# Reordering group 0's second product, one multiply, and the loads of q and v in a fused pooled-attention and GELU kernel

## Chip, cores, metric

One core of one Trainium2 chip. The metric is device time in microseconds (us) of one execution.

## What is computed

Attention whose keys and values are averaged over groups of 8 positions, then two matrix products with a GELU between them. Cut to what matters:

```python
# q, k, v: (8, 8, 576, 64); w_in: (512, 2048); w_out: (2048, 512), all float32
k_p = k.reshape(B, H, S // 8, 8, D).mean(axis=3)
v_p = v.reshape(B, H, S // 8, 8, D).mean(axis=3)
attn = softmax(q @ k_p^T / sqrt(D))           # 576 x 72 for each batch and head
x = (attn @ v_p) as (4608, 512)               # one row per token
out = gelu_tanh(x @ w_in) @ w_out             # (4608, 512)
```

## The kernel before

The tokens are worked through in nine groups of 512. Each group has a **first product** (64 big matmuls, line L411, and 16 GELUs on ScalarE) and a **second product** (64 big matmuls, L420: four row tiles of 128 tokens by 16 pieces of the sum). Beside the second product of group g runs the attention of batch g + 1, its matmuls put between the big ones at fixed places. Names in the profile: L281, L325 and L310 are scores (L310 those of the last 8 pooled positions, "remainder"), L301 and L336 attention times values, L354 the multiply by the softmax reciprocal, L426 the copy of a finished row tile out of PSUM. The "v sums" add v up over the 8 positions of a pooling group, on VectorE. PE is TensorE, DVE VectorE, ACT ScalarE, SP SyncE, POOL GpSimd.

```python
def load_next():                         # loads of batch g + 2, on GpSimd's queue
    if nb >= KX:                         # KX = 2, nb = g + 1
        nc.gpsimd.tensor_copy(out=gate, in_=eT[64:65, H - 1, 1, 0:2])   # holds the loads back
    ...
    load_k_dma(g + 2)
    ...
    load_v(g + 2, [nc.gpsimd])
    if nb >= KX:
        load_q(g + 2)
```

In groups 2 to 6, SyncE turns the loaded k and q by DMA transposes, k first (L190), then q (L269), each when its data are there. The second product of a group whose next batch is below 2, which is group 0 alone:

```python
at(4, v_half, 1, 0)                      # "at(m, ...)": put ahead of big matmul m
at(18, v_half, 1, 1)                     # second half of the v sums, on VectorE
pos = (6, 14, 21, 27, 34, 41, 48, 55, 61)
for i in range(len(ORDER) + 1):
    ...                                  # cut: at pos[i], scores i into banks 2, 3; values i - 1
                                         # into banks 4, 5 or 6, 7, in turn; exp and reciprocal
    if i:
        at(min(pos[i] + 9, ...), mult, *a)   # frees the two banks of "values i - 1"

seq = [(r, f) for r in range(4) for f in range(4)]      # first quarter of w_out, all row tiles
seq += [(r, 4 * f4 + f) for f4 in range(1, 4) for r in range(2) for f in range(4)]
seq += [(r, f) for r in (2, 3) for f in range(4, FO)]
```

Row tiles 2 and 3 keep the first quarter in banks 6 and 7, which are copied out (L653) so that the attention can have them; the rest of row tile 2 goes into row tile 0's bank, when that has been copied out (L426).

The softmax here doesn't subtract the row's maximum and nothing guards it: scores larger than these inputs give would overflow.

## Time and profile before

| | before |
|---|---|
| median of the first three runs | 301.47 us (301.32 to 301.6) |
| span of the profiled execution | 299.7 us, clock 1.0 |
| group 0's second product, first L420 to first L411 of group 1 | 34.92 to 53.87: 18.95 us |
| L310 of group 2 to L310 of group 3 | 99.29 to 130.63: 31.34 us |
| the same for the groups after | 31.08, 31.07, 31.08 us |

The last two rows are the easiest way to see a hole on an engine that is busy for 98% of the span, as TensorE is: groups 2 to 6 do the same work, so the distance between one instruction and its like in the next group is constant, and what is over 31.08 is a wait.

### The profile page before, as it was taken

Reading aid. Unit: us, or ns where it says so; the run is one execution under the profiler, and the core shown is the slowest. Engines: PE = TensorE matmul, PEld = TensorE weight load, DVE = VectorE, ACT = ScalarE, POOL = GpSimd, SP = SyncE. Lnnn points to the kernel's source line nnn. Section 1 sums busy time; section 2 is a strip of 40 time slices with the busy share of each in tenths; the row PEclk is TensorE's granted clock in tenths of the full one; section 3 lists DMA queues with packets and bytes.
Section 4 is the critical chain, followed back from the end, with each engine's and each line's share of the span. In section 5 each row is a group of like instructions: output and inputs, shape, how many; then the busy total and the mean of one; then the engine's idle time right before and its main releaser. Section 6 shows DMA issues by size and latency. Waiting matters only on the chain.

```text
span 299.7 us, 4384 instructions
## 1 busy us (share of the span) xinstructions
PE 293.4 (98%) x1525; PEld 151.4 (51%) x1525; DVE 153.1 (51%) x311; ACT 216.8 (72%) x408; POOL 38.0 (13%) x69
## 2 busy tenths in 40 slices
PE   8999999999999999999999999999999999999995
PEld 3565555554555455545554555455545555445443
DVE  4787577833675357716691669065924630111112
ACT  1697678879887997889878987798879887206500
POOL 2615100100500060006000410032000000000000
PEclk9999999999999999999999999999999999999999
DMA  7999999870899079846984499629961210121023
GB/s 225 259 225 297 248 216 182 213 146 15 188 264 180 16 171 255 160 77 147 250 180 83 101 258 200 103 50 254 236 120 40 71 37 0 37 70 36 0 54 89
DMA packets 38806, 43.11 MB, mean 144 GB/s; under 512 B 25536, under 2 KB 26176, under 8 KB 38656
## 3 DMA queue, kind: packets, MB, share of 16 engines
q0 software_dynamic: 8016, 24.39, 36.8%
q1 hardware_dynamic: 30064, 17.06, 25.6%
q10 hardware_dynamic: 704, 1.38, 1.4%
q8 instruction: 12, 0.20, 0.3%
q14 instruction: 10, 0.08, 0.1%
HBM read 36.70 MB, written 9.44 MB: 154 GB/s over the span
## 4 chain that ended last, share of the span: by engine, by line
PE 86%; DMA 7%; DVE 2%; issue 1%; POOL 1%; ACT 1%; POOLq 0%; SPq 0%; DVEq 0%
PE PS L411 37%; PE PS L420 36%; DMA qb<-in_q_dram 5%; PE PS L336 3%; PE PS L440 3%; PE PS L325 2%; DMA qT<-qb 2%; PE PS L661 1%; PE PS L281 1%; PE PS L310 1%; PE PS L377 1%; DMA eT<-er 1%; ACT e L288 1%; DVE xT L354 1%; PE PS L301 1%
## 5 line engine op out<-in xcount | busy, mean ns | idle before, releaser
L420 PE MATMUL PS<-w_out_b,gT 128*128 128x512 bf16 x560 | 136.9, 379 | 0.0
L411 PE MATMUL PS<-xT,w_in_b 128*128 128x512 bf16 x576 | 126.2, 379 | 0.0
L417 ACT ACTIVATE gT<-PS 128x512 bf16<-128x512 f32 x144 | 79.3, 609 | 44.3 <-PE PS L411 44.2
L411 PEld LDWEIGHTS <-w_in_b 128*128 128x128 bf16 x576 | 65.1, 113 | 58.8
L420 PEld LDWEIGHTS <-gT 128*128 128x128 bf16 x560 | 53.9, 97 | 51.4 <-issue 2.1
L354 DVE TENSOR_TENSOR xT<-PS,rc 64x288 bf16<-64x288 f32 x112 | 51.0, 455 | 19.7 <-ACT rc L346 17.1
L426 DVE COPY osb<-PS 128x512 f32<-128x512 f32 x33 | 22.8, 692 | 50.2 <-PE PS L420 41.9
L331 ACT ACTIVATE eT<-PS 64x576 bf16<-64x576 f32 x48 | 30.7, 640 | 0.6
L318 DVE COPY eT<-er 8x576 bf16<-8x576 bf16 x24 | 7.3, 303 | 41.4 <-ACT er L316 40.9
L343 ACT ACTIVATE ld<-PS 64x288 f32<-64x288 f32 x56 | 22.6, 403 | 5.8 <-PE PS L336 5.3
L346 ACT ACTIVATE rc<-ld 128x288 f32<-128x288 f32 x56 | 24.8, 443 | 1.8
L388 ACT ACT_TABLE_LOAD x17 | 21.8, 1283 | 3.6 <-issue 3.3
L344 ACT ACTIVATE ld<-PS 64x288 f32<-64x288 f32 x56 | 22.5, 402 | 1.4
L162 DVE TENSOR_TENSOR kt<-kt 128x1280 f32<-128x1280 f32 (+5 forms) x20 | 19.2, 959 | 5.6 <-DMA kt<-in_k_dram 4.9
L336 PE MATMUL PS<-eT,vp 72*128 72x288 bf16 x96 | 19.7, 285 | 0.0
L162 DVE TENSOR_TENSOR vt<-vt 128x512 f32<-128x512 f32 (+2 forms) x18 | 15.6, 865 | 2.7 <-DMA vt<-in_v_dram 2.3
L524 POOL COPY gate<-eT 1x2 bf16<-1x2 bf16 x5 | 0.9, 174 | 123.7 <-DMA eT<-er 123.7
L336 PEld LDWEIGHTS <-vp 72*128 72x128 bf16 x96 | 9.5, 98 | 11.3
L288 ACT ACTIVATE e<-PS 72x576 bf16<-72x576 f32 x16 | 9.9, 643 | 3.8 <-PE PS L281 3.6
L440 PE MATMUL PS<-idle 128*128 128x512 bf16 x31 | 10.0, 474 | 1.2 <-DVE idle L151 1.2
L325 PE MATMUL PS<-qT,kx 128*128 128x288 bf16 x48 | 9.8, 286 | 0.0
L562 DVE COPY kt<-gT 128x512 bf16<-128x512 bf16 x4 | 3.0, 744 | 11.6 <-ACT gT L417 11.6
(67 smaller groups left out, 132.3 us busy)
## 6 DMA issues: line engine op xcount, KB each, us to landing
out_dram<-osb SPq DMA_DIRECT2D x141, 64.0 KB
kt<-in_k_dram POOLq DMA_DIRECT2D x12, 512.0 KB, 7.0
vt<-in_v_dram POOLq DMA_DIRECT2D x12, 512.0 KB, 10.5
qb<-in_q_dram POOLq DMA_DIRECT2D x7, 576.0 KB, 14.8
w_out_b<-in_moe_w_out_dram POOLq DMA_DIRECT2D x4, 512.0 KB, 19.6
w_in_b<-in_moe_w_in_dram POOLq DMA_DIRECT2D x1, 1024.0 KB, 9.3
w_in_b<-in_moe_w_in_dram POOLq DMA_DIRECT2D x2, 512.0 KB, 12.3
kt<-in_k_dram POOLq DMA_DIRECT2D x1, 1024.0 KB, 15.9
```

The source lines that it names most:

```text
L162: nc.vector.tensor_tensor(out=o, in0=a, in1=b, op=ALU.add)
L331: nc.scalar.activation(out=eT[0:64, 2 * pr:2 * pr + 2, c, :], in_=PS[64 * c:64 * c + 64, 2:4, :CH], func=ACT.Exp, scale=1.0 / 64.0)
L336: nc.tensor.matmul(out=PS[:, bank + x, :CH], lhsT=window(vps[b % 2], 2 * pr + x), rhs=eT[:, 2 * pr + x, c, :], start=True, stop=True)
L343: nc.scalar.activation(out=ld[0:64], in_=PS[64:128, bank, :CH], func=ACT.Ln)
L344: nc.scalar.activation(out=ld[64:128], in_=PS[0:64, bank + 1, :CH], func=ACT.Ln)
L346: nc.scalar.activation(out=rc, in_=ld, func=ACT.Exp, scale=-1.0)
L354: nc.vector.tensor_tensor(out=xT[rows, pr, col:col + CH], in0=PS[rows, bank + x, :CH], in1=rc[rows], op=ALU.mult)
L388: nc.scalar.preload_act_table_set(name)
L411: nc.tensor.matmul(out=PS[:, h_bank(g, fo), :], lhsT=w, rhs=xT[:, ko, r0:r0 + GROUP], start=(ko == 0), stop=(ko == KO - 1))
L417: nc.scalar.activation(out=gTs[g][:, fo, :], in_=PS[:, h_bank(g, fo), :], func=ACT.Gelu_apprx_tanh)
L420: nc.tensor.matmul(out=PS[:, bank], lhsT=gTs[g][:, fo, r * 128:(r + 1) * 128], rhs=w_out_b[:, fo], start=(fo == first), stop=(fo == last))
L426: nc.vector.tensor_copy(out=osb, in_=PS[:, bank])
```

## The change

The intent: VectorE should free attention's banks sooner in group 0, and q, which must pass through a transpose, should be on the chip sooner in later groups. `plan` says behind which of the 16 GELUs VectorE gets the next batch's k sums (`kk`) and v sums (`vv`). The multiply with `i == 3` moves from matmul 36 to matmul 34; row tile 0's output copy is queued behind matmul 35, so the multiply passes in front of it.

```diff
-            load_v(g + 2, [nc.gpsimd])
             if nb >= KX:
                 load_q(g + 2)
+            load_v(g + 2, [nc.gpsimd])
...
-                plan = {0: kk, 7: vv[:1], 8: vv[1:]}
+                plan = {0: kk, 11: vv[:1], 12: vv[1:]}
...
-                at(18, v_half, 1, 1)
+                at(12, v_half, 1, 1)
...
-                    at(min(pos[i] + 9, 62 if i < len(ORDER) else 65), mult, *a)
+                    at(min(pos[i] + (7 if i == 3 else 9), 62 if i < len(ORDER) else 65), mult, *a)
...
-            seq = [(r, f) for r in range(4) for f in range(4)]
+            seq = [(r, f) for r in (0, 2, 3, 1) for f in range(4)]
```

## The prediction

> **What bounds the kernel now.** I read the page first, then TensorE's waits, then the timelines around each wait.
>
> ```profile
> span 299.7 us, 4384 instructions
> PE 293.4 (98%) x1525; PEld 151.4 (51%) x1525; DVE 153.1 (51%) x311; ACT 216.8 (72%) x408; POOL 38.0 (13%) x69
> ```
>
> TensorE is occupied for 98% of the span at a granted clock of 1.0, so the change can only give back holes in TensorE's stream. The view of waits, for TensorE alone, has these:
>
> ```profile
> PE PS L440 <- DVE idle L151: 1.2, 1, 1.2
> PE PS L281 <- ACT qT L259: 0.6, 1, 0.6
> PE PS L301 <- DVE xT L354: 0.4, 2, 0.2
> PE PS L310 <- DMA qT<-qb: 0.2, 1, 0.2
> ```
>
> The first two lie in the first 11 us, which the change doesn't touch. The other two (0.6 us together) are what it aims at. The listed waits are a little too small, because a matmul's drawn length overlaps the next one's. Starts are better: a run of 64 big matmuls takes 13.81 us in the chain, 0.216 us each, and an undisturbed pair of L301 (attention times values) delays the next matmul by 0.245 us. TensorE's timeline in group 0's second product:
>
> ```profile
> 42.20 0.41 PE L281 MATMUL PS<-qT,kT 128*72 128x288 bf16 x2
> 42.58 0.28 PE L301 MATMUL PS<-e,vp 72*128 72x288 bf16 x1
> 43.07 0.28 PE L301 MATMUL PS<-e,vp 72*128 72x288 bf16 x1 [0.21 <-DVE xT L354]
> 45.20 1.75 PE L420 MATMUL PS<-w_out_b,gT 128*128 128x512 bf16 x7
> 46.79 0.41 PE L281 MATMUL PS<-qT,kT 128*72 128x288 bf16 x2
> 47.06 0.28 PE L301 MATMUL PS<-e,vp 72*128 72x288 bf16 x1
> 47.55 0.28 PE L301 MATMUL PS<-e,vp 72*128 72x288 bf16 x1 [0.21 <-DVE xT L354]
> ```
>
> First hole: the first L301 starts 0.38 us after the L281 pair instead of 0.25 (0.13 lost), and the second 0.49 us after the first instead of 0.12 (0.37 lost): **0.50 us**. Second hole: again 0.37, plus 0.02, plus 0.08 in the run at 45.20, which took 1.75 us where other runs of seven take 1.67: **0.47 us**. Why is in VectorE's timeline:
>
> ```profile
> 38.18 0.69 DVE L653 COPY osb<-PS 128x512 f32<-128x512 f32 x1
> 39.53 0.69 DVE L653 COPY osb<-PS 128x512 f32<-128x512 f32 x1 [0.67 <-PE PS L420]
> 40.26 1.15 DVE L162 TENSOR_TENSOR vt<-vt 128x512 f32<-128x512 f32 x2
> 41.44 0.60 DVE L162 TENSOR_TENSOR vp<-vt 64x128 bf16<-64x128 f32 x2
> 42.08 1.92 DVE L354 TENSOR_TENSOR xT<-PS,rc 64x288 bf16<-64x288 f32 x4
> 45.83 0.69 DVE L426 COPY osb<-PS 128x512 f32<-128x512 f32 x1 [1.84 <-PE PS L420]
> 46.55 0.94 DVE L354 TENSOR_TENSOR xT<-PS,rc 64x288 bf16<-64x288 f32 x2
> ```
>
> VectorE works in program order: partial copy of row tile 2, partial copy of tile 3 (it waits 0.67 us for TensorE), second half of the v sums, and only then, at 42.08, the multiplies that free the banks of the next L301 pair. At 46.55 the multiply stands behind an output copy.
>
> The third hole is in group 3. A row-tile run of two ends and L310 (remainder scores) waits for the transposed q; the SyncE timeline gives the cause, beside group 5 as one that doesn't wait:
>
> ```profile
> 122.67 1.32 SPq L190 DMA_TRANSPOSE kx<-kz  x1
> 125.97 2.67 SPq L269 DMA_TRANSPOSE qT<-qb  x1
> ...
> 185.09 1.31 SPq L190 DMA_TRANSPOSE kx<-kz  x1
> 186.50 4.36 SPq L269 DMA_TRANSPOSE qT<-qb  x1
> ```
>
> L310 starts 0.79 us after the L420 pair before it (129.84 to 130.63), against 0.53 in group 2 (98.76 to 99.29): **0.26 us**. In group 3 the transpose of q can't be issued at 124.0, when that of k is done, but at 125.97, when q lands (the chain of waits has q's load there, 15.80 us, then 4.61 us of transpose).
>
> [...]the bar at 125.97 is 2.67 us, the landing comes after 4.61.[...] the trace has 692 for the output's add and a mean of 455 for L354.[...]
>
> **The change part by part.** It adds and removes no instruction. The order of instructions, old against new, differs on GpSimd (q before v, five groups), on VectorE in one place (in group 0 two multiplies move in front of an output copy), and on TensorE in the row tile that a matmul takes. The new places of the v sums (11 and 12 for 7 and 8, 12 for 18) change no engine's order, so I count zero for them.
>
> 1. Row tiles 0, 2, 3, 1. Tiles 2 and 3 finish their quarter after matmuls 7 and 11 instead of 11 and 15. Matmul 11 ended at about 38.14 (the copy began at 38.18). VectorE finishes the first half of the v sums at 38.11, copies tile 2 to 38.87 and tile 3 to 39.59 without a wait, does the second half of the v sums (1.79 us) to 41.40, and two multiplies to 42.35 (their reciprocal was there at 40.83). L301 needs them at 42.45 and 42.57. The first hole closes: **-0.50 us**, with a thin margin of 0.2 us.
>
> 2. The multiply in front of the copy. ScalarE is occupied without a break from 38.85 to 44.70 and isn't sped up, so the reciprocal for this multiply still comes at 44.70. Multiplies 44.74 to 45.68. The copy of row tile 0, ready at 45.32 now, runs behind them, 45.72 to 46.41. Row tile 2's next matmul uses that bank. It would start at 46.00 (0.50 sooner than an undisturbed 46.50) but must wait for about 46.46. So at this point 0.45 of part 1 is lost again, TensorE being 0.11 ahead of the old 46.57. Then L301 finds its banks free: 0.37 and some hundredths saved. Part 1 and 2 together: 0.11 + 0.37 = **-0.48 us**, not 0.97. From there ScalarE's and VectorE's chains move along by the same amount; I find no later wait (the next multiply is done at 48.1, needed at 48.9).
>
> 3. q before v. Its issue moves up by the 1.28 us of the two v issues, and its data no longer queue behind 1 MB of v. q should land before k's transpose is issued, so q's goes out right behind, as in group 5: 6.35 us before L310 there, against 4.66 in group 3, 5.66, 5.80 and 6.02 in groups 2, 4 and 6. The transpose took 4.61, so none waits: **-0.26 us**. v lands last, when q did: 125.97 in group 3 instead of before 122.66. Its sums take 2.8 us on VectorE, to 128.8; they are first needed by L336 at 133.6, and VectorE's next other work is at 132.63. No cost.
>
> Sum: -0.48 - 0.26 = -0.74 us. 301.47 - 0.74 = **300.7 us**.
>
> **The rivals.**
> - *Both holes of group 0 close and no copy waits* (the reciprocal comes sooner than I think, or the bank is free earlier): -0.97 - 0.26, 300.2 us. Against it: ScalarE's unbroken row up to 44.70.
> - *The reordering only moves the wait*: the copy behind the multiply holds the bank for as long as the multiply did, and part 1's margin of 0.2 us proves too thin. Group 0 gains 0 to 0.2, in all 301.1 to 301.4 us. For it: VectorE's work between 38 and 46.5 is the same, in another order.
> - *The transposes collide with v.* The first transpose of q, issued at 46.42 among other loads, landed at 54.16, after 7.7 us. With 7.7 us and issue 6.35 us ahead, L310 would wait 1.4 us in each of five groups: plus 7 us, 308 us. Against it: v ends at about the time at which q ended before, so at most 2 us of the transpose overlaps, and the margin is 6.35 - 4.61 = 1.7 us.
> - *q was hidden anyway.* Four of five groups show no wait, so part 3 may be worth 0.0 in the timed runs: 301.0 us.
>
> **Range and chances.** 300.7 is the sum; the low end of 300.1 is the first rival with a little of the runs' spread (301.32 to 301.6), the high end of 301.5 is the second and the fourth together. 2% is 6 us, five times all the holes that can be closed, so faster by that is next to impossible; slower needs the collision in every group.
>
> **What would show it.** In the new profile: the copies of tiles 2 and 3 back to back from 38.2, the first multiply at about 41.4, no wait at the L301 pair near 42.5; the output copy at about 45.7 and a hole of 0.4 us ahead of the matmul that follows (row tile 2, near 46.4), put down to that copy; no hole at the L301 near 46.9; group 1 starting near 53.5 instead of 54.03. In groups 2 to 6 q's transpose starts within 0.2 us of the end of k's issue and L310 has no wait for it; VectorE waits about 3 us for v without TensorE noticing. The prediction is wrong if TensorE waits for v's sums at L336, if L310 waits in several groups, or if group 0 gains under 0.2 or over 0.9 us.

## The result

300.82 us (median of 6, 300.5 to 301.21) against 301.39 (median of 6, 301.09 to 301.65). Ratio 0.9982, 95% interval 0.9969 to 0.9994: 0.18%, or 0.54 us. Ratios here are of means, so they are not quite the ratio of the medians quoted beside them.

The page of the kernel after, its first lines, and TensorE's waits after:

```profile
span 299.1 us, 4388 instructions
PE 293.1 (98%) x1525; PEld 151.3 (51%) x1525; DVE 153.3 (51%) x311; ACT 216.7 (72%) x408; POOL 38.1 (13%) x69
```

```profile
PE PS L440 <- DVE idle L151: 1.2, 1, 1.2
PE PS L281 <- ACT qT L259: 0.6, 1, 0.6
PE PS L420 <- DVE osb L426: 0.3, 1, 0.3
```

In the second list the columns are who waited for whom, us in total, times, longest. Both L301 waits and the L310 wait are gone; a wait of L420 for the output copy is new. TensorE's timeline after (start, duration, engine, line, what, count):

```profile
42.33 0.41 PE L281 MATMUL PS<-qT,kT 128*72 128x288 bf16 x2
42.57 0.41 PE L301 MATMUL PS<-e,vp 72*128 72x288 bf16 x2
...
44.83 1.46 PE L420 MATMUL PS<-w_out_b,gT 128*128 128x512 bf16 x6
46.58 0.38 PE L420 MATMUL PS<-w_out_b,gT 128*128 128x512 bf16 x1 [0.30 <-DVE osb L426]
46.80 0.41 PE L281 MATMUL PS<-qT,kT 128*72 128x288 bf16 x2
47.04 0.41 PE L301 MATMUL PS<-e,vp 72*128 72x288 bf16 x2
```

The L301 pairs are whole again (one row of two in place of two rows of one). The matmul at 46.58 should follow six others that began at 44.83, at 44.83 + 6 x 0.216 = 46.13: 0.45 us late. VectorE's timeline after:

```profile
38.16 1.28 DVE L654 COPY osb<-PS 128x512 f32<-128x512 f32 x2
39.46 1.15 DVE L162 TENSOR_TENSOR vt<-vt 128x512 f32<-128x512 f32 x2
...
41.29 0.94 DVE L354 TENSOR_TENSOR xT<-PS,rc 64x288 bf16<-64x288 f32 x2
...
44.87 0.94 DVE L354 TENSOR_TENSOR xT<-PS,rc 64x288 bf16<-64x288 f32 x2 [0.93 <-ACT rc L346]
45.84 1.29 DVE L426 COPY osb<-PS 128x512 f32<-128x512 f32 x2
```

The partial copies run back to back, the multiplies begin at 41.29 (before: 42.08), and the output copy now stands behind a multiply that waited for ScalarE. Group 0's second product takes 35.04 to 53.49, 18.45 us: **0.50 less**. L310 comes every 31.08 us in all groups: **0.26 less**. That is 0.76; the span is only 0.6 shorter because in this execution the second product of group 0 began 0.12 us later (35.04 for 34.92), which is start-up.

SyncE's transposes after, in groups 2 and 3, and then VectorE's v sum in group 3:

```profile
91.21 2.71 SPq L190 DMA_TRANSPOSE kx<-kz  x1
94.01 2.78 SPq L269 DMA_TRANSPOSE qT<-qb  x1
...
122.29 1.32 SPq L190 DMA_TRANSPOSE kx<-kz  x1
123.71 3.55 SPq L269 DMA_TRANSPOSE qT<-qb  x1
```

```profile
123.80 1.95 DVE L162 TENSOR_TENSOR vt<-vt 128x1024 f32<-128x1024 f32 x2 [1.45 <-DMA vt<-in_v_dram]
```

q's transpose goes out 0.1 us after k's. From issue to landing the page has a median of 10.7 us for q's loads and 12.4 for v's, for 14.8 and 10.5 before; in group 3 q's took 11.51 us with v (two loads of 512 KB) behind it, and 15.80 before, when it landed at 125.95, after those of v at 119.49 and 122.31. VectorE waits 1.45 us for v (about 3 was forecast), and TensorE's waits name no v.

### The profile page after: what moved, and what is told of

It is laid out like the page before. It is cut to its first block, busy times and chain, and to the rows that moved or that the text cites. A ratio compares the mean times of both kernels' runs of the same rounds, so it can differ in the third digit from the quotient of the medians.

```text
span 299.1 us, 4388 instructions
## 1 busy us (share of the span) xinstructions
PE 293.1 (98%) x1525; PEld 151.3 (51%) x1525; DVE 153.3 (51%) x311; ACT 216.7 (72%) x408; POOL 38.1 (13%) x69
## 4 chain that ended last, share of the span: by engine, by line
PE 95%; ACT 2%; DVE 1%; issue 0%; DVEq 0%
PE PS L411 42%; PE PS L420 39%; PE PS L336 4%; PE PS L440 3%; PE PS L325 2%; PE PS L281 1%; PE PS L662 1%; ACT e L288 1%; PE PS L310 1%; PE PS L377 1%; PE PS L249 1%; PE PS L363 0%; PE PS L301 0%; DVE xT L354 0%; ACT rc L346 0%
## 5 line engine op out<-in xcount | busy, mean ns | idle before, releaser
L420 PE MATMUL PS<-w_out_b,gT 128*128 128x512 bf16 x560 | 137.0, 379 | 0.3 <-DVE osb L426 0.3
L420 PEld LDWEIGHTS <-gT 128*128 128x128 bf16 x560 | 53.9, 97 | 50.7 <-issue 1.3
## 6 DMA issues: line engine op xcount, KB each, us to landing
vt<-in_v_dram POOLq DMA_DIRECT2D x12, 512.0 KB, 12.4
qb<-in_q_dram POOLq DMA_DIRECT2D x7, 576.0 KB, 10.7
```

The source lines that it names most:

```text
L420: nc.tensor.matmul(out=PS[:, bank], lhsT=gTs[g][:, fo, r * 128:(r + 1) * 128], rhs=w_out_b[:, fo], start=(fo == first), stop=(fo == last))
```

## The experiments

Two questions. In group 0: which part gave the 0.50 us, and is the new hole where the rest went? In later groups: was the wait for q real in every execution, or an accident of the one profiled? Two numbers are read from every trace: the length of group 0's second product, and the distance of L310 from group 2 to group 3. "Lead" is the time from the issue of q's transpose to L310 in group 3. It isn't margin: how long the transpose takes to land changes too, from 4.61 to 5.97 us in the kernels before and after (see the margin of part 3, below).

| run | group 0, us | L310 distance, us | lead, us | median, us | before, same chip | ratio (95%) |
|---|---|---|---|---|---|---|
| before | 18.95 | 31.34 | 4.66 | 301.39 | | |
| after | 18.45 | 31.08 | 6.27 | 300.82 | 301.39 | 0.9982 (0.9969 to 0.9994) |
| e1_rows | 18.45 | 31.08 | 5.85 | 301.19 | 301.2 | 0.9993 (0.9979 to 1.0007) |
| e2_mult | 18.56 | 31.08 | 5.90 | 301.05 | 301.2 | 0.9993 (0.9978 to 1.0009) |
| e3_q_first | 18.96 | 31.08 | 6.28 | 301.31 | 301.36 | 1.0001 (0.9987 to 1.0014) |
| e4_rows_mult | 18.44 | 31.08 | 6.08 | 300.81 | 301.2 | 0.9985 (0.997 to 1.0001) |
| e5_pos40 | 17.99 | 31.08 | 6.28 | 300.29 | 301.2 | 0.9967 (0.9954 to 0.9981) |
| e6_pos40_late_mult | 18.68 | 31.08 | 6.28 | 301.1 | 301.36 | 0.9995 (0.9983 to 1.0008) |
| e9_pos40_v_first | 18.00 | 31.08 | 5.16 | 300.58 | 301.34 | 0.9974 (0.9962 to 0.9987) |
| e10_pos40_q_first | 18.22 | 31.08 | 6.28 | 300.65 | 301.34 | 0.9974 (0.996 to 0.9987) |
| e11_before_again | 18.96 | 31.08 | 5.26 | 301.72 (one run) | | |

e7 and e8, which delay the loads, stand below. All gave the right result, and every timed run was fast (e11's state is unknown, as of any single run). In the timed columns the intervals are about 0.4 us to each side, as large as the effects; verdicts on single parts rest on the traces.

### Rows alone

```diff
 # against before
-at(18, v_half, 1, 1)
+at(12, v_half, 1, 1)
-seq = [(r, f) for r in range(4) for f in range(4)]
+seq = [(r, f) for r in (0, 2, 3, 1) for f in range(4)]
```

> Only the row order 0, 2, 3, 1 in group 0, the multiply left behind the output copy, v in front of q. Measure: group 0's second product, from the first L420 matmul to the first L411 of group 1, 18.95 us before (34.92 to 53.87) and 18.45 after the whole change (35.04 to 53.49). Theory (multiply and copy only swap places, so the multiply's own move is worth nothing once the rows are reordered): the copy is done at about 46.0, no hole ahead of row tile 2's matmul, and a hole of about 0.4 us at the L301 near 46.9 put down to xT; 18.46 us. Rival (each part is worth its own hole, rows 0.50 and multiply 0.47, and the copy's hole comes from the multiply): 18.45 here too, but then the multiply alone must be worth nothing. Group 3's hole of about 0.26 at L310 may be there. Time 300.9, against 301.4 before.

Measured: 18.45 us, so the rows alone give all of the 0.50. The hole sits at L301, where it was before the change, but the first one is gone (TensorE's timeline, then VectorE's):

```profile
47.54 0.28 PE L301 MATMUL PS<-e,vp 72*128 72x288 bf16 x1 [0.21 <-DVE xT L354]
```

```profile
45.82 0.69 DVE L426 COPY osb<-PS 128x512 f32<-128x512 f32 x1 [1.52 <-PE PS L420]
46.55 0.94 DVE L354 TENSOR_TENSOR xT<-PS,rc 64x288 bf16<-64x288 f32 x2
```

The copy is in front of the multiply, so L301 pays; in the whole change it is the other way round, and L420 pays.

### The multiply alone

```diff
 # against before
-at(min(pos[i] + 9, 62 if i < len(ORDER) else 65), mult, *a)
+at(min(pos[i] + (7 if i == 3 else 9), 62 if i < len(ORDER) else 65), mult, *a)
```

> Only the multiply in front of the output copy in group 0, row tiles 0, 1, 2, 3, v in front of q. Theory: the hole of 0.50 near 42.5 stays (multiplies begin at 42.1), the copy is then released by TensorE at 45.8 and not by the multiply, so row tile 2's matmul starts as before, and the L301 near 47 has no hole: 18.95 - 0.39 = 18.56 us for group 0's second product. So alone the multiply is worth 0.39, with the rows about 0. Rival (multiply worth nothing, it only moves the wait to the copy): 18.95. Time 301.0.

Measured: 18.56 us, as worked out: alone it is worth 0.39. In the old row order TensorE finishes row tile 0 half a microsecond later, after the multiply is done, so the copy isn't delayed by it (it starts at 45.97, released by TensorE; the multiplies end at 45.82).

### Rows and multiply, v still in front of q

```diff
 # against e1_rows
-at(min(pos[i] + 9, 62 if i < len(ORDER) else 65), mult, *a)
+at(min(pos[i] + (7 if i == 3 else 9), 62 if i < len(ORDER) else 65), mult, *a)
```

> Rows and multiply, v still in front of q. Theory: group 0's second product 18.45 us, as in the whole change, with a hole of 0.46 ahead of row tile 2's matmul put down to the output copy; group 3's L310 may still wait (0.26). If parts 1 and 3 are independent the time is 0.0 to 0.26 above the whole change: 300.9 to 301.1.

Measured: 18.44 us. **The two parts don't add**: 0.50 and 0.39 alone, 0.51 together. One multiply pair (0.94 us) and one copy (0.69 us) fall due on VectorE at the same time, and TensorE needs both within half a microsecond; swapping them decides only which matmul waits. And with v still in front of q, L310 had no wait in group 3, although the expectation allowed for one.

### Closing the hole that is left: score and value group at matmul 40

```diff
 # against after
-pos = (6, 14, 21, 27, 34, 41, 48, 55, 61)
+pos = (6, 14, 21, 27, 34, 40, 48, 55, 61)
```

> The whole change, and the sixth group of score and value matmuls moved from matmul 41 to 40, in front of row tile 2's first matmul, so that TensorE has 0.49 us of other work while VectorE copies the bank out. Theory (the remaining hole is the copy behind the multiply, and the multiply is done at 45.8, in time for the moved L301 at 46.4): the hole of 0.46 closes, no other opens; group 0's second product 18.45 - 0.46 = 17.99 us; ScalarE's unbroken row goes on through 46.75; time 0.46 below the whole change, about 300.4. Rival (ScalarE sets the pace of this stretch, so that a hole closed here opens again at a later L301 or at group 1's first product): 18.3 to 18.45 us.

Measured: 17.99 us, and a ratio of 0.9967 to before; no hole is left in group 0's second product. TensorE's timeline of this run:

```profile
44.70 1.46 PE L420 MATMUL PS<-w_out_b,gT 128*128 128x512 bf16 x6
45.99 0.41 PE L281 MATMUL PS<-qT,kT 128*72 128x288 bf16 x2
46.24 0.41 PE L301 MATMUL PS<-e,vp 72*128 72x288 bf16 x2
46.48 1.89 PE L420 MATMUL PS<-w_out_b,gT 128*128 128x512 bf16 x8
```

While VectorE copies the bank out (45.70 to 46.39), TensorE does work that the multiply (44.73 to 45.67) has already released. So the rival, that ScalarE sets the pace of the stretch, falls: the gain stayed to the end of the group.

### The same place, multiply behind the copy

```diff
 # against e5_pos40
-at(min(pos[i] + (7 if i == 3 else 9), 62 if i < len(ORDER) else 65), mult, *a)
+at(min(pos[i] + 9, 62 if i < len(ORDER) else 65), mult, *a)
```

> The whole change with the sixth score and value group at matmul 40, but the multiply back behind the output copy. Theory (the multiply's place is worth nothing only because row tile 2's matmul needs the copy next; once L301 comes first it is worth a lot): multiplies 46.05 to 47.0, L301's two matmuls wait to about 46.5 and 47.1, then row tile 2: group 0's second product 18.6 to 18.7 us, 0.65 more than with the multiply sooner. Rival (order of multiply and copy immaterial): 18.0 us.

Measured: 18.68 us, 0.69 more; both matmuls of the moved L301 pair wait.

```profile
46.52 0.28 PE L301 MATMUL PS<-e,vp 72*128 72x288 bf16 x1 [0.15 <-DVE xT L354]
47.02 0.28 PE L301 MATMUL PS<-e,vp 72*128 72x288 bf16 x1 [0.21 <-DVE xT L354]
```

The early multiply, worth nothing beside the new row order, is worth 0.69 once TensorE's order matches VectorE's. With this place and the multiply late, group 0 is even 0.23 us longer than with the rows alone.

### q in front of v, alone

```diff
 # against before
-load_v(g + 2, [nc.gpsimd])
 if nb >= KX:
     load_q(g + 2)
+load_v(g + 2, [nc.gpsimd])
-plan = {0: kk, 7: vv[:1], 8: vv[1:]}
+plan = {0: kk, 11: vv[:1], 12: vv[1:]}
```

> Only q loaded in front of v. Theory: the hole of 0.26 us in front of L310 in group 3 closes, no other group has one, group 0's second product stays at 18.95 us; VectorE waits 0.7 to 1.5 us for v in each group, which nobody waits for; time 301.4 - 0.26 = 301.1 at best, and 0.0 if timed executions mostly had no such wait. Rival (the transposes collide with v): L310 waits in some groups, time over 301.4.

Measured: no wait at L310 in any group, but no gain in time either (ratio 1.0001). In its trace TensorE's start-up had a wait of 0.5 us for k's sums that the first trace hadn't, another sign of how much of the spread lies in the first microseconds. By itself inconclusive to 0.4 us; the next three runs were made for this.

### Order of q and v on the best kernel, and the kernel before once more

```diff
 # e9_pos40_v_first against e5_pos40: load_v in front of load_q again, v sums at 7 and 8
 # e10_pos40_q_first: e5_pos40 again, on the same chip
 # e11_before_again: the kernel before
```

> Rows, multiply and matmul place 40, with v in front of q as before. Run beside the same with q in front. In the profiles of the three runs with v in front of q and the loads at their usual time (rows, multiply, both), L310 did not wait for q in any group, against 0.26 us in the kernel before's. Theory (the order of q and v is worth 0.26 us in some executions and nothing in most): within 0.15 us of the run with q in front, group 0's second product 17.99 us. Rival (it is worth 0.26 us in each): 0.26 us longer, with a wait at L310 in group 3.

> The run of matmul place 40 again, on the chip of its partner with v in front: 300.3 to 300.5, 1.0 below the kernel before; no wait at L310; group 0's second product 17.99 us.

> The kernel before, looked at once more: is the wait of 0.26 us at L310 in group 3 in every execution? Theory (it is not): L310 comes 31.08 us after L310 of the group before in all of groups 3 to 6. Rival: 31.34 us again in group 3.

Measured: 300.58 with v first, 300.65 with q first, both 0.9974 of before: no difference. These times alone know the difference only to about 0.4 us (an estimate from the spread of the six and five runs), so they don't exclude 0.26; the traces decide. The kernel before, looked at again, has L310 at 99.70 and 130.78, 31.08 apart (the largest distance in its later groups is 31.12). Of six traces with v first at the usual time (before, again, e1, e2, e4, e9), **one** has the wait in group 3, and it is the one that the prediction was made from; the other five, with leads of 5.16 to 6.08, don't wait there. The expectation for e10 missed: 18.22 for 17.99. A run of seven L420 took 1.90 us there where others took 1.68; it holds matmul 32, the first to need the last quarter of w_out, and this trace has TensorE waiting 0.4 us for w_out's first quarter at the start of the product too. The chain of work in this trace names the cause:

```profile
23.92 20.41 DMA w_out_b<-in_moe_w_out_dram
44.33 0.04 issue
44.37 0.59 PE PS L420 x2
```

The last quarter of w_out landed at 44.33, and matmul 32 began at 44.37, 0.44 us after the one before it in place of 0.22: the missing 0.23. In e5's trace the same load landed at 42.63, in e9's at 44.17, 0.05 us before matmul 32. So with VectorE's holes closed, the load of w_out can be what limits group 0: it was in one of the three traces with place 40 and the early multiply.

### All loads 2.6 us later, v first against q first

```diff
 # on the kernel before (e7) and on the kernel after (e8)
-nc.gpsimd.tensor_copy(out=gate, in_=eT[64:65, H - 1, 1, 0:2])
+nc.gpsimd.tensor_copy(out=gate, in_=eT[0:1, 4, 0, 0:2])
-at(3, load_next)
+at(34, load_next)
```

> The kernel before, with all loads for groups 3 to 7 issued about 2.6 us later (the gate waits for a later score exponential). It enlarges what the order of q and v is worth. Theory (q's landing sets L310): L310 waits in every one of groups 2 to 6, by 2.6 us less the slack of each (0.3 to 1.5 us): 1 to 3 us each, together 6 to 9 us; time 307 to 310. Rival (q is hidden anyway, with a margin of microseconds): 301.4 to 302.

> The whole change, with all loads for groups 3 to 7 issued about 2.6 us later, as in the run before it. Theory (q in front of v gives q's transpose about 4 us): q still lands by the time at which k's transpose is out, L310 waits for nothing or up to 0.5 us per group where the transposes run beside v, v's sums end at about 129 in group 3, ahead of L336: 300.8 to 303, so 5 us or more below the same delay with v first. Rival (the transposes collide with v, or v comes too late for L336): the same loss as with v first, 307 or more.

Measured: 308.28 us (306.53 to 309.14, ratio 1.0223, interval 1.0191 to 1.0255) with v first, 301.95 (301.47 to 302.03, ratio 1.0017, interval 1.0004 to 1.0031) with q first. TensorE's waits, of e7 and then of e8:

```profile
PE PS L310 <- DMA qT<-qb: 6.3, 5, 2.1
```

```profile
PE PS L310 <- DMA qT<-qb: 1.1, 2, 0.9
```

From L310 of group 1, which has no such wait, to L310 of group 6, e7 needs 161.82 us and e8 156.46, against 5 x 31.08 = 155.40. In e7 SyncE issues q's transpose 1.57 to 2.77 us after it is done with that of k, waiting for q; in e8 0.10 to 0.11 us. So q in front of v does what it is meant to, 5.4 us over five groups here. It buys room for late loads, which this kernel at its usual load time doesn't draw on.

One number of e8 missed: up to 0.5 us of wait per group was expected, and group 5 had 0.95. q's transpose was issued at 185.92 in group 5, and L310 ran at 193.22, 7.30 us later:

```profile
193.22 0.44 PE L310 MATMUL PS<-qT,kx 128*16 128x288 bf16 x8 [0.95 <-DMA qT<-qb]
```

v was still landing beside it, since VectorE's sum waited for v until 188.14. But v landed beside q's transpose in all five groups of e8 (its sum began 1.68 to 2.72 us after the transpose's issue), and in groups 2 to 4 the transpose took 4.65, 5.38 and 5.42 us to land, no longer than the 4.68, 5.53 and 5.36 of the kernel after; only in groups 5 and 6 was it longer (7.16 for 5.97, 5.78 for 5.38). So a collision with v isn't shown; what made group 5's transpose late stays open.

## Why the prediction was right, step by step

**What bounds it**: right. Every saving seen is a hole on TensorE closed, and none is larger than the holes listed.

**Part 1, rows, 0.50**: right. The rows alone give 0.50, and the partial copies stand back to back at 38.16 to 39.44.

**Part 2, multiply in front of the copy**: right in mechanism and size. Predicted were a hole of 0.45 us ahead of row tile 2's matmul, put down to the copy, and 0.48 for both parts; measured 0.45 and 0.50. The prediction booked it as a loss and a gain of nearly the same size; the runs put it more sharply: on top of the rows the multiply is worth 0.01, alone 0.39, and with the next group of scores in front 0.69.

**Part 3, q before v, 0.26**: right for the execution that it was read from, wrong as a part of the time. The failing step is "none waits: -0.26 us": the wait of 0.26 was taken for a property of the kernel, while five of six traces of kernels with v first don't have it. In its place the traces show 0.0 in most executions, and the times of e9 and e10 agree with that, though they can't exclude 0.26. The fourth rival, q hidden anyway, was the right one for those five traces. The total held because 0.50 and 0.74 both lie well inside the range: measured 0.54. As far as part 3 goes, that was luck.

**The margin of part 3**: wrong in size, though no time shows it. The step that failed here is "The transpose took 4.61, so none waits". 4.61 us was measured in group 3, where q's transpose was issued 3.30 us after that of k; the prediction set it against a lead of 6.35 us with q's right behind k's, 1.7 us to spare. (6.35 is 6.29 by the timeline: for groups 2, 4, 5 and 6 the prediction took L310's start from the chain, which has it 0.07 us later.) q's transpose does go out within 0.1 us of the end of k's issue in all five groups, with leads of 6.21 to 6.29 us in groups 3 to 6. But in these two traces it took longer to land where it followed k's sooner: in the kernel before 4.61 us at 3.30 us after the issue of k's, 4.85 at 2.11, 4.92 at 1.94, 5.12 at 1.74, and 5.93 at 1.41 (groups 3, 2, 4, 6, 5); in groups 3 to 6 of the kernel after, at 1.41 to 1.49 us, 5.53, 5.36, 5.97 and 5.38. The distance isn't all of it: in e7, where L310 waited for q in all five groups, L310 ran 4.64 to 4.70 us after the issue of q's transpose in groups 2, 3, 4 and 6, at 3.21 to 4.53 us after the issue of k's, but 5.33 us after it in group 5, at 3.47. So in the kernel after it lands only 0.74, 0.91, 0.32 and 0.83 us ahead of L310, and at the usual load time the order of q and v hardly moves its landing: in group 3 it is 0.74 to 0.86 us ahead of L310 in five traces with q first, and 0.61 to 0.85 in the five with v first that don't wait. (The chain prints a landing only where L310 waited for it; the others were read from the semaphore updates in the traces, which give the chain's figures where both exist.)

**Part 3's smaller numbers**: in group 2 the transpose of k was on SyncE for 2.71 us, for 1.56 before, so q's went out later, and its lead is only 98.90 - 94.01 = 4.89 us, for 5.59 before. q landed there 0.21 us ahead of L310, for 0.74 before; over all traces at the usual load time 0.21 to 0.54 with q first (five traces) and 0.49 to 0.81 with v first (six). The change took a little of the margin there; why is open. v was to land at 125.97 in group 3; its sum began at 123.80.

**Places of the v sums**: counted as zero. Setting them back to 18, 7 and 8 in the changed kernel gives, instruction for instruction and wait for wait, the same program on all five engines (only numbers in some buffers' names differ), so this is shown without a run.

## What to carry to other kernels

Where two results fall due on one engine at once and the bottleneck needs both, moving one in front of the other only changes who waits (here it was worth 0.01 us); give the bottleneck its own work in the order in which the results come, which here made a move worth nothing into one worth 0.69 us. The time that a transfer took in one place isn't its time in another: q's transpose took 4.61 us to land where it was issued 3.3 us after that of k, and 5.36 to 5.97 at 1.4 to 1.5 us. A wait of a few tenths of a microsecond behind a DMA, seen in one trace and in one of several like groups, is an accident until a second trace shows it. To learn whether a reordering of loads buys margin, delay all loads and see which order breaks first.
